# Equal dense shares for steps with a PV pair, and LayerNorm roots taken four blocks at a time, in a fused attention and GLU kernel

## The chip, the cores and the metric

The kernel runs on one core of a Trainium2 chip. The metric is the device time of one execution in microseconds (us). Each kernel is run several times; medians and ranges of all runs are given. The span of a profile (first to last instruction) is some 1.7 us less than the time of the same execution.

PE is TensorE, ACT ScalarE, DVE VectorE, POOL GpSimd, SP the engine that issues most transfers.

## The reference, cut to what matters

```python
xn = layernorm(x)                      # x: 2048 x 640
q, k, v = split(xn @ wqkv)             # 32 heads of 20
p = softmax(mask(q @ k.T * 20**-0.5))  # causal, window of 256
A = (p @ v) @ wo
B = (sigmoid(xn @ w_gate) * (xn @ w_up)) @ w_down   # inner size 1536
return x + A + B
```

## The kernel before

The 2048 rows are four chunks of 512. Attention runs in 76 score steps: 16 for chunk 0, 20 for each of the others (four wide steps and a full one for every two groups of heads). A step is 16, 24 or 32 small score matmuls into one PSUM tile `ps`, one exponential over all of it on ACT, and masks on POOL. While ACT works, PE is fed from a queue of dense work ("fill"): projections, gate and up blocks, the down projection, the output projection. The PV products of two groups (`acc`, 2 x 28 matmuls in chunk 0, 2 x 48 later) come due at fixed steps.

```python
def scores(c, step):
    pt = pp.tile([P, HG, PTW], BF16, name="pT")
    ps = ps_s.tile([P, HG, CW], FP32, name="ps")      # one buffer
    ...                                               # score matmuls
    nc.scalar.activation(out=pt[:, :, 0:CW], in_=ps, func=EXP, scale=SCALE)
    ...                                               # three masks on GpSimd
```

The gate and up blocks: tanh on ACT writes `th`, of which there is one buffer; DVE makes `h` of it. Engines take their instructions in the order in which they were recorded, so where a block stands between the steps also fixes where its tanh and its h stand.

```python
tp = pool("tp", 1)
...
th = tp.tile([P, CW], FP32, name="th")
nc.scalar.activation(out=th, in_=pg, func=TANH, scale=0.5)
yield 5 * MM
...                                                   # five up matmuls into pu
nc.vector.scalar_tensor_tensor(out=h, in0=th, scalar=1.0, in1=pu, op0=ADD, op1=MULT)
yield 5 * MM
```

The loop that decides how much dense work a step gets. `fill.pull(ns)` emits pieces until their cost is at least `ns`; `PV` is the charge per PV group. After a PV pair DVE transposes both accumulators; scaling one group (reciprocal, products, a transpose) is emitted behind each of the next two pieces.

```python
PV = 740
...
for t, (c, k, step) in enumerate(todo):
    ...
    for group in due.get(t, []):
        pv(*group, parts.pop(group))
    made = (step, scores(c, step))
    ...
    sums = [PV * len(due.get(x, [])) for x in range(t + 1, min(last, len(todo) - 1) + 1)]
    credit += (fill.left(label) + sum(sums)) / (last - t) - sum(sums[:1])
    credit = fill.pull(credit)
```

A PV pair is emitted ahead of the next scores, so it lies at the end of a step, behind that step's dense work.

The softmax here doesn't subtract the row's maximum and nothing guards it: scores larger than these inputs give would overflow.

## Time and profile before

| | kernel before |
|---|---|
| time, median of 3 runs | 320.13 us (319.48 to 321.1) |
| profiled span | 317.9 us |
| PE / ACT / POOL / DVE busy | 96% / 61% / 51% / 50% |
| first and last score step begin at | 31.5 and 292.5 us |

The useful reading is by steps: the distance from the start of one step's first score matmul to the start of the next, less the price of the work in the step (the prices are worked out in the prediction below). What is over is PE's wait in that step. "Excess" below always means this.

### The profile page before, as it was taken

The numbers are of one execution on the slowest core, as the hardware profiler recorded it, in microseconds if no ns is written. First come the engines' busy times: TensorE is split into PE (matmuls) and PEld (weight loads), VectorE is DVE, ScalarE is ACT, GpSimd is POOL, SyncE is SP. The second block draws the span as 40 slices with busy tenths as digits, with TensorE's granted clock in tenths as the row PEclk, the third lists the DMA queues.
The fourth block names the chain that finished last, engine by engine and source line by source line (L and its number), as shares of the span: only waits on it lengthen the run. The fifth ranks groups of instructions, "written<-read, shape, count | busy, mean of one in ns | idle before, by whom it ended". The sixth has DMA issues, their size and how long they took to land.

```text
span 317.9 us, 10527 instructions
## 1 busy us (share of the span) xinstructions
PE 306.4 (96%) x4627; PEld 176.5 (56%) x4666; DVE 158.0 (50%) x313; ACT 192.6 (61%) x179; POOL 161.0 (51%) x257
## 2 busy tenths in 40 slices
PE   8999999999999999999999999999999999998996
PEld 2654444556567655554566656554466655453675
DVE  3531568637685344277651644345262717272054
ACT  5724878597754458766754457867667567868100
POOL 3000487667685554737565463735547474747000
PEclk9999999999999999999999999999999999999999
DMA  7985999537704254520424024600000010000002
GB/s 260 371 293 176 337 386 127 206 110 241 155 23 62 66 173 124 169 76 0 41 40 50 25 104 141 207 7 2 0 5 23 23 37 8 2 4 0 3 2 83
DMA packets 34669, 33.08 MB, mean 104 GB/s; under 512 B 10016, under 2 KB 34080, under 8 KB 34592
## 3 DMA queue, kind: packets, MB, share of 16 engines
q1 hardware_dynamic: 34192, 32.14, 35.8%
q8 instruction: 36, 0.59, 0.8%
q10 hardware_dynamic: 432, 0.28, 0.3%
q14 instruction: 9, 0.07, 0.1%
HBM read 21.00 MB, written 10.26 MB: 98 GB/s over the span
## 4 chain that ended last, share of the span: by engine, by line
PE 76%; ACT 10%; POOL 6%; issue 3%; DMA 3%; DVE 1%; ACTq 0%
PE y L416 14%; PE pqk L291 12%; PE pu L402 11%; PE pg L395 11%; ACT pT L469 8%; PE ps L464 7%; PE y L423 6%; PE pv L318 6%; PE acc L496 6%; POOL pT L472 5%; PE d L416 2%; DMA xnT<-xn 2%; POOL rstd L258 1%; DMA xc<-in_A_x_dram 1%; PE d L423 1%
## 5 line engine op out<-in xcount | busy, mean ns | idle before, releaser
L472 POOL TENSOR_SCALAR_AFFINE_SELECT pT<-pT 128x512 bf16<-128x512 bf16 (+2 forms) x192 | 146.8, 796 | 131.0 <-ACT pT L469 130.9
L469 ACT ACTIVATE pT<-ps 128x2048 bf16<-128x2048 f32 x76 | 142.7, 1878 | 68.6 <-PE ps L464 63.8
L406 DVE SCALAR_TENSOR_TENSOR h<-th,pu 128x512 bf16<-128x512 f32 x48 | 32.9, 685 | 62.7 <-PE pu L402 37.7
L395 PE MATMUL pg<-xnT,wg 128*128 128x512 bf16 x224 | 58.3, 380 | 1.3 <-issue 0.6
L402 PE MATMUL pu<-xnT,wu 128*128 128x512 bf16 x227 | 58.8, 380 | 0.6
L416 PE MATMUL y<-wd,h 128*128 128x320 bf16 (+1 forms) x348 | 49.9, 297 | 0.0
L291 PE MATMUL pqk<-xnT,wqkv 128*128 128x512 bf16 x190 | 45.8, 381 | 0.7 <-DMA xnT<-xn 0.2
L416 PEld LDWEIGHTS <-h 128*128 128x128 bf16 x396 | 36.8, 98 | 14.3
L398 ACT ACTIVATE th<-pg 128x512 f32<-128x512 f32 x48 | 28.6, 595 | 17.1 <-PE pg L395 14.3
L464 PEld LDWEIGHTS <-kT 20*64 20x64 bf16 x1856 | 21.2, 103 | 27.2 <-issue 25.2
L402 PEld LDWEIGHTS <-wu 128*128 128x128 bf16 x240 | 22.0, 98 | 25.7 <-DMA wu<-in_B_w_up_dram 0.4
L464 PE MATMUL ps<-qT,kT 20*64 20x128 bf16 (+4 forms) x1856 | 32.5, 239 | 3.5 <-ACT pT L469 3.4
L395 PEld LDWEIGHTS <-wg 128*128 128x128 bf16 x240 | 21.7, 98 | 24.9 <-issue 0.6
L506 DVE STREAM_TRANSPOSE t<-acc 128x512 f32<-128x512 f32 x32 | 21.8, 708 | 23.9 <-PE acc L496 23.9
L291 PEld LDWEIGHTS <-wqkv 128*128 128x128 bf16 x200 | 22.3, 119 | 18.6 <-issue 1.5
L427 DVE SCALAR_TENSOR_TENSOR xn<-y,xc 128x320 bf16<-128x320 f32 (+1 forms) x29 | 14.0, 485 | 29.4 <-PE y L423 29.4
L518 DVE TENSOR_TENSOR on<-t,rec 128x320 bf16<-128x320 f32 (+4 forms) x48 | 27.2, 567 | 1.1
L496 PE MATMUL acc<-pT,v 128*32 128x64 bf16 (+3 forms) x1376 | 23.9, 223 | 1.4 <-ACT pT L469 1.1
L496 PEld LDWEIGHTS <-v 128*32 128x32 bf16 x1376 | 19.1, 97 | 9.2 <-issue 4.6
L318 PE MATMUL pv<-wqkv,xnT 128*128 128x320 bf16 x160 | 23.6, 299 | 0.0
L423 PE MATMUL y<-wo,oc 128*128 128x320 bf16 (+1 forms) x145 | 21.6, 297 | 0.0
L295 DVE CAST st<-pqk 128x512 bf16<-128x512 f32 x20 | 13.8, 691 | 12.6 <-PE pqk L291 12.6
(46 smaller groups left out, 151.1 us busy)
## 6 DMA issues: line engine op xcount, KB each, us to landing
qT<-sq SPq DMA_DIRECT2D x7, 512.0 KB, 5.8
sq<-st SPq DMA_DIRECT2D x20, 128.0 KB, 3.5
sk<-st SPq DMA_DIRECT2D x20, 128.0 KB, 2.7
out_dram<-xn SPq DMA_DIRECT2D x15, 160.0 KB, 1.8
kT<-sk SPq DMA_DIRECT2D x4, 512.0 KB, 6.7
wg<-in_B_w_gate_dram SPq DMA_DIRECT2D x2, 960.0 KB, 7.6
wu<-in_B_w_up_dram SPq DMA_DIRECT2D x2, 960.0 KB, 9.6
xc<-in_A_x_dram SPq DMA_DIRECT2D x3, 640.0 KB, 5.4
```

The source lines that it names most:

```text
L291: nc.tensor.matmul(ps, lhsT=wt[:, m, :], rhs=xnT[c][:, d, :], start=(d == 0), stop=(d == DC - 1))
L318: nc.tensor.matmul(ps[:, 0:HALF], lhsT=xnT[c][:, d, s * P:(s + 1) * P], rhs=wqkv[:, d, 2 * D + hf * HALF:2 * D + (hf + 1) * HALF], start=( ...
L395: nc.tensor.matmul(pg, lhsT=part(wg, d, f), rhs=xnT[c][:, d, :], start=(d == 0), stop=(d == DC - 1))
L398: nc.scalar.activation(out=th, in_=pg, func=TANH, scale=0.5)
L402: nc.tensor.matmul(pu, lhsT=part(wu, d, f), rhs=xnT[c][:, d, :], start=(d == 0), stop=(d == DC - 1))
L406: nc.vector.scalar_tensor_tensor(out=h, in0=th, scalar=1.0, in1=pu, op0=ADD, op1=MULT)
L416: nc.tensor.matmul(y[:, 0:cut[1] - cut[0]], lhsT=ht[c, f][:, s * P:(s + 1) * P], rhs=wd[:, f, cut[0]:cut[1]], start=(f == 0), stop=False)
L423: nc.tensor.matmul(y[:, 0:cut[1] - cut[0]], lhsT=oc[c, m][:, s * P:(s + 1) * P], rhs=wo[:, m, cut[0]:cut[1]], start=False, stop=(m == DC - 1))
L464: nc.tensor.matmul(ps[hf * U:(hf + 1) * U, i, col * U:(col + n) * U], lhsT=qk["k", kc, g // GH][32 * i:32 * i + DH, g % GH, key:key + U], ...
L469: nc.scalar.activation(out=pt[:, :, 0:CW], in_=ps, func=EXP, scale=SCALE)
L472: nc.gpsimd.affine_select(out=out, in_=in_, pattern=[[0, HG], [0, n], [sign, width]], compare_op=GE, fill=0.0, base=base, channel_multipli ...
L496: nc.tensor.matmul(acc[32 * i:32 * i + 32, q * U:(q + n) * U], lhsT=v[:, h * VW:h * VW + 32], rhs=pt[:, i, col * U:(col + n) * U], start=( ...
```

## The change

Its intent: give every score step of a stage the same dense work, whether it also has a PV pair or not; and take LayerNorm's reciprocal root once for four blocks instead of once per block, with the normalisation a piece of work later, so that DVE waits less for it.

```diff
-    def rstd_block(mv):
-        rstd = lnp.tile([P, 1], FP32, name="rstd")
-        nc.gpsimd.tensor_scalar(out=rstd, in0=mv[:, 1:2], scalar1=EPS, scalar2=None, op0=ADD)
-        nc.gpsimd.tensor_tensor(out=rstd, in0=rstd, in1=neghalf, op=POW)
-        return rstd
+    def rstd_blocks(mvs):
+        rstds = lnp.tile([P, SBC], FP32, name="rstds", bufs=1)
+        nc.gpsimd.tensor_scalar(out=rstds, in0=mvs[:, :, 1], scalar1=EPS, scalar2=None, op0=ADD)
+        nc.gpsimd.tensor_tensor(out=rstds, in0=rstds, in1=neghalf, op=POW)
+        return rstds
 ...
-        for k in range(SBC + 4):
-            ...   # statistics of block k, root of k-1, norm of k-3, turn of k-4
+        for s in range(SBC):
+            ln_block(c, s, mvs[:, s, :])
+            if s == SBC - 1:
+                rstds = rstd_blocks(mvs)
+            yield 0
+        yield 0
+        for s in range(SBC):
+            norm_block(c, s, mvs[:, s, :], rstds[:, s:s + 1])
+            yield 0
+            if turn:
+                turn_block(c, s)
 ...
-    PV = 740
 ...
-        sums = [PV * len(due.get(x, [])) for x in range(t + 1, min(last, len(todo) - 1) + 1)]
-        credit += (fill.left(label) + sum(sums)) / (last - t) - sum(sums[:1])
+        credit += fill.left(label) / (last - t)
         credit = fill.pull(credit)
```

(Cut: the signatures of the helpers, and the constant of -0.5 widened to four columns.)

More of the change, by code (lines that the diff above doesn't have):

```diff
@@ L225 @@
     make_identity(nc, ident)
-    neghalf = const.tile([P, 1], FP32, name="neghalf")
+    neghalf = const.tile([P, SBC], FP32, name="neghalf")
     nc.gpsimd.memset(neghalf, -0.5)
@@ L245, in ln_half, with ln_mv, ln_block @@
         return stats
-    def ln_mv(stats):
-        mv = lnp.tile([P, nc.vector.BN_AGGR_DIM], FP32, name="mv")
+    def ln_mv(stats, mv=None):
+        if mv is None:
+            mv = lnp.tile([P, nc.vector.BN_AGGR_DIM], FP32, name="mv")
         nc.vector.bn_aggr(out=mv, in_=stats)
         return mv
-    def ln_block(c, s):
-        return ln_mv(ln_half(c, s, 1, ln_half(c, s, 0)))
-    def rstd_block(mv):
-        rstd = lnp.tile([P, 1], FP32, name="rstd")
-        nc.gpsimd.tensor_scalar(out=rstd, in0=mv[:, 1:2], scalar1=EPS, scalar2=None, op0=ADD)
-        nc.gpsimd.tensor_tensor(out=rstd, in0=rstd, in1=neghalf, op=POW)
-        return rstd
+    def ln_block(c, s, mv=None):
+        return ln_mv(ln_half(c, s, 1, ln_half(c, s, 0)), mv)
+    def rstd_blocks(mvs):
[3 more added lines that the diff above has]
+        return rstds
     def norm_block(c, s, mv, rstd):
@@ L336, in g_norms @@
         new_xnT(c)
-        mv, rstd = {}, {}
-        for k in range(SBC + 4):
-            if k < SBC:
-                mv[k] = ln_block(c, k)
-            if 0 <= k - 1 < SBC:
-                rstd[k - 1] = rstd_block(mv[k - 1])
-            if k < SBC:
-                yield 0
-            if 0 <= k - 3 < SBC:
-                norm_block(c, k - 3, mv[k - 3], rstd[k - 3])
-                yield 0
-            if turn and 0 <= k - 3 - 1 < SBC:
-                turn_block(c, k - 3 - 1)
+        mvs = lnp.tile([P, SBC, nc.vector.BN_AGGR_DIM], FP32, name="mvs", bufs=1)
+        for s in range(SBC):
[9 more added lines that the diff above has]
+                turn_block(c, s)
     def g_turns(c):
@@ L634 @@
     proj_v(0, 3, 1, act)
-    nc.scalar.activation(out=scr, in_=neghalf, func=EXP)
+    nc.scalar.activation(out=scr, in_=neghalf[:, 0:1], func=EXP)
     for _ in g_qk(0):
```

## The prediction

> **What bounds the kernel now.** I read the page's totals first, then the waits of TensorE (PE), then the timeline around the steps in which PE stood still, and last the list of PE matmuls by form.
>
> ```profile
> PE 306.4 (96%) x4627; PEld 176.5 (56%) x4666; DVE 158.0 (50%) x313; ACT 192.6 (61%) x179; POOL 161.0 (51%) x257
> ...
> PEclk9999999999999999999999999999999999999999
> ...
> PE 76%; ACT 10%; POOL 6%; issue 3%; DMA 3%; DVE 1%; ACTq 0%
> ```
> PE is busy nearly all the time at full clock and has 76% of the chain that ended last; no other engine is over 61%. So only what PE does not fill can be won. How much is that? The waits give the kind:
> ```profile
> PE ps L464 <- ACT pT L469: 3.4, 5, 1.3
> ...
> PE acc L496 <- ACT pT L469: 1.1, 4, 0.5
> ...
> ACT th L398 <- DVE h L406: 1.0, 1, 1.0
> ```
> Five times the next scores (ps) wait for the exponential (pT), because ps has one buffer; four times the PV product (acc) waits for it. PE's idle time is understated, since a matmul's end is modelled and overlaps the next: the mean of a 512-column matmul is 380 ns, yet five of them take 1.08 us in the chain, 0.216 each. So I measured from starts. Each of the 76 score steps is: scores, exponential on ScalarE (ACT), masks on GpSimd (POOL), and dense work on PE meanwhile. From the timeline a step without waits is 0.46 us for scores and switching, plus 0.216 per 512-column matmul, 0.136 per 320-column one, plus 1.46 for a PV pair of chunks 1 to 3 (2 x 48 matmuls) or about 1.1 for one of chunk 0 (2 x 28). That sum reproduces most of the 75 step lengths to 0.02 us. Where it does not, PE waited:
> ```profile
> 244.14 0.43 PE L464 MATMUL ps<-qT,kT 20*64 20x128 bf16 x32
> 244.50 0.99 PE L416 MATMUL y<-wd,h 128*128 128x320 bf16 x6
> 244.73 1.88 ACT L469 ACTIVATE pT<-ps 128x2048 bf16<-128x2048 f32 x1 [1.02 <-PE ps L464]
> 245.42 0.74 PE L496 MATMUL acc<-pT,v 128*32 128x320 bf16 x40
> 246.66 0.97 PE L496 MATMUL acc<-pT,v 128*32 128x128 bf16 x56 [0.50 <-ACT pT L469]
> 247.56 0.44 PE L464 MATMUL ps<-qT,kT 20*64 20x320 bf16 x24
> ```
> This PV step has six dense matmuls. Its last 56 PV matmuls read the exponential of the same step (done at 246.61), so the step lasts 3.42 us for 2.74 of work: 0.68 idle. The other kind, in the last chunk:
> ```profile
> 268.74 0.59 DVE L518 TENSOR_TENSOR on<-t,rec 128x256 bf16<-128x256 f32 x1
> 269.25 0.68 DVE L406 SCALAR_TENSOR_TENSOR h<-th,pu 128x512 bf16<-128x512 f32 x1
> 270.02 0.60 ACT L398 ACTIVATE th<-pg 128x512 f32<-128x512 f32 x1 [1.02 <-DVE h L406]
> 270.51 1.87 ACT L469 ACTIVATE pT<-ps 128x2048 bf16<-128x2048 f32 x1
> 272.44 0.43 PE L464 MATMUL ps<-qT,kT 20*64 20x320 bf16 x24 [0.60 <-ACT pT L469]
> ```
> VectorE (DVE) scaled the two PV groups before it got to h; th has one buffer, so tanh waited for h; the exponential stands behind tanh and came late; PE stood.
>
> Step by step, the waits before are: thin steps (dense work under the 2.56 us that scores plus exponential take) 0.74 + 0.44 + 0.46 = 1.64; PV steps with too little dense work 0.14 + 0.42 + 0.68 + 0.42 + 0.36 = 2.02; the DVE lag above, twice, 0.68 + 1.42 = 2.10; the two steps around the normalisation of chunk 1, 0.55; scattered rest 0.47. Together 6.8 us, 2% of the time: a ceiling on the gain.
>
> **What the Trainium skill says.** "Perfetto Trace Analysis", Identifying the Most-Contended Engine, warns that matmul busy share does not tell how near PE is to its limit because matmuls are pipelined; the trace agrees (380 ns booked, 216 ns spacing). The same page, Tensor Engine Instruction, calls ACT, DVE and GPSIMD strict FIFO; the tanh at 270.02 holding up the exponential at 270.51, whose scores had been issued by 269.4, agrees. "SBUF — State Buffer", Who interferes with whom, says a DVE instruction with two SBUF inputs contends with a GpSimd instruction that reads SBUF; the 320-column scaling takes 0.49 us where it starts before the masks (235.10) and 0.95 under them (250.19), which fits, though it does not prove it. "GPSIMD Engine Reference", Elementwise — side-by-side cycle accounting, names two software dispatch hops per instruction; the trace has 0.593 us for a power of one column, so I take that as nearly all fixed.
>
> **The change part by part.**
> Shares. The matmuls are the same, 4666 on both sides; only their places move. The old rule charged 740 ns per PV group against a step's share, so PV steps got little dense work (one block of five) and the others two or three blocks. The new rule gives all steps of a stage the same dense work, PV or not. I took the new PE order from the instruction listing and priced every step with the constants above.
> - PV steps of chunks 1 to 3 now hold at least 10 wide or 16 narrow dense matmuls: at least 0.46 + 2.16 + 1.46 = 4.08 us, above the 3.42 floor. The 2.02 goes to 0.
> - Thin steps: three become two, one with ten 320-column matmuls (1.82 of work, 0.74 idle), one with twelve (2.09, 0.46): 1.64 to 1.20.
> - Last chunk: each step becomes gate block, up block. After a PV step the DVE order is then two transposes, scaling, h, scaling, h, instead of h, both scalings (3.0 and 3.7 us), h. From PV end at A: the transposes end at A+0.84, the first scaling by A+2.8, h at A+3.8, the second scaling by A+5.8, h at A+6.5; the tanh that needs that buffer stands behind an exponential that ends at about A+7.7. No wait: 2.10 to 0. The plain steps here are 2.62 us against a floor of 2.56, so the margin is only 0.06.
> LayerNorm. Twelve pairs on POOL (12 x (0.224 + 0.593) = 9.8 us) become three. With four columns in place of one I estimate 0.85 a pair, 2.6 in all: 7.2 us off POOL, which at 51% is not the bound, so worth nothing directly. But the norms come about two dense pieces later. In chunk 1 the root now waits for all four statistics and for the masks of the next step: exponential done 43.0, masks to 45.0 (1.95), root to 45.85, first norm to 46.35 instead of 43.63. h of that pair is queued behind it (47.05), and tanh, so the next exponential slips 0.2. Then the last two norms and the scalings of chunk 0's first pair share DVE: norm 49.35, h 50.05, scaling 51.0, norm 51.45, scaling 53.7, h 54.4. The tanh before the next exponential waits to 55.05, where scores are ready at 53.85: about 1.1 us of PE idle. With the 0.1 before it, 1.2. The four transposing DMAs (first issued at 43.66 before, about 2.1 us apart, last landed 56.08) start near 46.4; PE wants them at about 57.2 by then. I allow 0.3. So 0.55 becomes 1.5.
> Slots: in two places an output tile now follows at once on the add that frees its PSUM buffer, without scores between: 0.1 each; with the old rest, 0.7.
> Sum after: 1.20 + 0 + 0 + 1.5 + 0.7 = 3.4, against 6.8. Saved 3.4 of 320.13: **316.7 us**, 1.1% less. Head and tail (before the first scores at 31.5, after the last at 292.5) are untouched.
>
> **Rivals.**
> 1. The new chunk-1 wait is larger: transposes finish in DMA order behind the 1.9 MB load of wd, whose packets run to about 49.5, and three of four landings came after 54. If SP issues them from 46.4 at 2.1 us each and the last lands 5.6 us after its issue at 52.7, PE waits 1 us more: 317.7 to 318.5. For it: PE already waited 0.2 for the last one. Against: in chunks 2 and 3, without such a load, issue takes 1.25 and landing 2.6.
> 2. The uniform 2.62 us steps become bound by the exponential: ACT has 1.88 + 0.60 per step plus the hand-over of 0.66 (end of exponential to start of the next), so any tanh that overhangs by over 0.06 us lengthens the step. Over ten steps at 0.1 that is 1 us: 317.7. Against: nine such two-block steps before ran at 2.62.
> 3. Only the shares matter and the norms cost nothing, as POOL's relief (four root pairs fell between masks at 42.6 to 47.8 before) lets PV masks finish early: then the 1.5 returns to 0.3 and it is 315.5.
> 4. Nothing gained, because work moved from PV steps makes other steps thin. The priced list speaks against it: only two steps are under 2.56.
>
> **Range and chances.** Runs of the kernel before spread 1.6 us. Rivals 1 and 2 together give 319, rival 3 and a little luck 315. Range 314.9 to 319.0. Faster by over 2% needs 313.7, less than a full removal of all but 0.4 us of waits: 3%. Slower by over 2% needs over 6 us of new waits: 2%. Within 2%: 95%.
>
> **What would show it.** Right: no wait of acc for the exponential; PV steps of about 4.1 us; no tanh waiting for h in the last chunk, where step lengths repeat 2.62 and 4.08; six root instructions on POOL, about 2.6 us in all; two steps of 2.56 in the third out-projection; a tanh near 54 that waits for h, and a late exponential after it. Wrong: first QK projection of chunk 1 waiting over 1 us for the transposes; last-chunk steps above 2.7; a DVE that waits for the root longer than the 6.5 us of before with PE idle behind it.

## The result, and the profile after

The changed kernel takes **316.19 us** (median of 4 runs, 315.95 to 317.66), the kernel before 320.62 (4 runs, 319.48 to 321.52) in the same rounds. The ratio is 0.9873, 95% interval 0.9827 to 0.992: within 2%. A ratio is the mean time of one kernel's fast runs over that of the other's of the same rounds, so it is not quite the ratio of the medians. The prediction was 316.7, range 314.9 to 319.0. The two profiled spans differ by 3.2 us: 3.0 of it is excess in the steps, 0.2 an earlier start (first scores at 31.3 us in place of 31.5). The medians differ by 4.4, so some 1 us between them is not in these two profiles.

The totals and the chain that ended last, from the page of the changed kernel:

```profile
span 314.7 us, 10543 instructions
...
PE 307.0 (98%) x4666; PEld 175.7 (56%) x4666; DVE 157.6 (50%) x313; ACT 192.6 (61%) x179; POOL 154.7 (49%) x239
...
PE 91%; ACT 4%; POOL 1%; DMA 1%; issue 1%; DVE 1%; ACTq 0%
```

Busy times moved by less than 1 us but for POOL's 6; what changed is the chain, which runs through PE for 91% of the span where it was 76%. PE's waits in the changed kernel (who waited for whom: us in total, times, longest):

```profile
PE ps L464 <- ACT pT L469: 1.9, 3, 0.8
PE pwarm L235 <- DVE st L164: 1.3, 1, 1.3
PE pt L272 <- DVE xn L264: 0.7, 1, 0.7
PE y L416 <- issue: 0.6, 1, 0.6
PE pu L402 <- DVE h L406: 0.3, 1, 0.3
```

The wait of `acc` for the exponential is gone. Five waits of the scores are three: two thin steps and one near chunk 1's norms. New are a wait of 0.6 for "issue", of which more below, one for h, and one in the start (`pt` for `xn`). The kernel before had four waits for "issue", of 0.2 at most, all at `pg`, of whose 240 matmuls 16 are missing from its trace. A PV step of the last chunk and the step after it, from the timeline of the changed kernel:

```profile
260.09 0.43 PE L464 MATMUL ps<-qT,kT 20*64 20x128 bf16 x32
260.45 1.25 PE L395 MATMUL pg<-xnT,wg 128*128 128x512 bf16 x5
260.69 1.88 ACT L469 ACTIVATE pT<-ps 128x2048 bf16<-128x2048 f32 x1 [1.54 <-PE ps L464]
261.54 1.24 PE L402 MATMUL pu<-xnT,wu 128*128 128x512 bf16 x5
...
262.72 1.52 PE L496 MATMUL acc<-pT,v 128*32 128x320 bf16 x96
...
264.17 0.43 PE L464 MATMUL ps<-qT,kT 20*64 20x320 bf16 x24
...
266.79 0.43 PE L464 MATMUL ps<-qT,kT 20*64 20x320 bf16 x24
```

The exponential ends at 262.57, before the first PV matmul at 262.72, so all 96 run in one go, where the kernel before had a break between 40 and 56 of them. The step lasts 4.08 us, the next 2.62; both are their work to 0.01.

Two steps near chunk 1's norms are over their work, by 0.54 and 0.92 us. The second, in the same timeline:

```profile
50.92 1.22 DVE L264 TENSOR_SCALAR xn<-xc,mvs,rstds 128x640 bf16<-128x640 bf16 x1
...
53.37 0.48 DVE L518 TENSOR_TENSOR on<-t,rec 128x128 bf16<-128x128 f32 x1
...
53.77 0.67 DVE L406 SCALAR_TENSOR_TENSOR h<-th,pu 128x512 bf16<-128x512 f32 x1
53.78 1.25 PE L395 MATMUL pg<-xnT,wg 128*128 128x512 bf16 x5
54.54 0.60 ACT L398 ACTIVATE th<-pg 128x512 f32<-128x512 f32 x1 [1.76 <-DVE h L406]
...
55.03 1.87 ACT L469 ACTIVATE pT<-ps 128x2048 bf16<-128x2048 f32 x1
...
56.95 0.42 PE L464 MATMUL ps<-qT,kT 20*64 20x320 bf16 x16 [0.84 <-ACT pT L469]
```

It is the picture that the prediction showed for the last chunk of the kernel before, moved here: DVE is at a norm and at the scaling, h comes at 53.77, tanh waits for h, the exponential stands behind tanh, the next scores wait for the exponential.

One wait was not foreseen. PE and its weight loads (PEld) in the step at 88 us of the changed kernel:

```profile
88.37 0.45 PE L416 MATMUL y<-wd,h 128*128 128x320 bf16 x2
...
89.43 0.39 PEld L416 LDWEIGHTS <-h 128*128 128x128 bf16 x4 [0.95 <-issue]
89.43 0.72 PE L416 MATMUL y<-wd,h 128*128 128x320 bf16 x4 [0.62 <-issue]
```

In the middle of a group of twelve matmuls, whose operands had all been there for long, even the weight load stops until 89.43; no semaphore is named. The step is 0.79 us over its work.

Excess by kind in the profiles of both kernels, in us, beside what was predicted of the changed one:

| | before | predicted after | after |
|---|---|---|---|
| thin steps | 1.64 | 1.20 | 1.17 |
| PV steps | 2.02 | 0 | 0 |
| DVE lag, last chunk | 2.10 | 0 | 0 |
| near chunk 1's norms | 0.55 | 1.5 | 1.46 |
| step at 88 us | 0 | not foreseen | 0.79 |
| rest | 0.47 | 0.7 | 0.33 |
| sum | 6.78 | 3.4 | 3.75 |

### The profile page after: what moved, and what is told of

It reads as the page before. It is cut to its first block, busy times and chain, and to the rows that moved or that the text cites.

```text
span 314.7 us, 10543 instructions
## 1 busy us (share of the span) xinstructions
PE 307.0 (98%) x4666; PEld 175.7 (56%) x4666; DVE 157.6 (50%) x313; ACT 192.6 (61%) x179; POOL 154.7 (49%) x239
## 4 chain that ended last, share of the span: by engine, by line
PE 91%; ACT 4%; POOL 1%; DMA 1%; issue 1%; DVE 1%; ACTq 0%
PE pg L395 16%; PE pu L402 15%; PE y L416 15%; PE pqk L292 14%; PE ps L464 8%; PE pv L319 7%; PE acc L496 7%; PE y L423 5%; ACT pT L469 4%; PE d L416 2%; DMA xc<-in_A_x_dram 1%; POOL pT L472 1%; PE d L423 1%; POOL rstds L259 0%; PE pt L272 0%
## 5 line engine op out<-in xcount | busy, mean ns | idle before, releaser
L402 PE MATMUL pu<-xnT,wu 128*128 128x512 bf16 x240 | 59.8, 380 | 0.3 <-DVE h L406 0.3
L395 PE MATMUL pg<-xnT,wg 128*128 128x512 bf16 x240 | 59.9, 380 | 0.0
L416 PE MATMUL y<-wd,h 128*128 128x320 bf16 (+1 forms) x348 | 50.6, 297 | 0.6 <-issue 0.6
L518 DVE TENSOR_TENSOR on<-t,rec 128x320 bf16<-128x320 f32 (+4 forms) x48 | 25.1, 523 | 1.1
L496 PE MATMUL acc<-pT,v 128*32 128x64 bf16 (+3 forms) x1376 | 23.0, 223 | 0.0
```

The lines of the kernel that those rows point to most:

```text
L395: nc.tensor.matmul(pg, lhsT=part(wg, d, f), rhs=xnT[c][:, d, :], start=(d == 0), stop=(d == DC - 1))
L402: nc.tensor.matmul(pu, lhsT=part(wu, d, f), rhs=xnT[c][:, d, :], start=(d == 0), stop=(d == DC - 1))
L416: nc.tensor.matmul(y[:, 0:cut[1] - cut[0]], lhsT=ht[c, f][:, s * P:(s + 1) * P], rhs=wd[:, f, cut[0]:cut[1]], start=(f == 0), stop=False)
L496: nc.tensor.matmul(acc[32 * i:32 * i + 32, q * U:(q + n) * U], lhsT=v[:, h * VW:h * VW + 32], rhs=pt[:, i, col * U:(col + n) * U], start=( ...
```

## The experiments

Three questions were open. Is it the shares or the LayerNorm part that earns the time? Are the three mechanisms (the floor of PV steps, tanh behind h, thin steps) causes or only companions? What is the wait at 88 us? The theory is the prediction's; the main rival is that relief of POOL by the batched roots earns a good part. Four kernels ran on one chip, three on a second, two on a third, five rounds each but for one with three; all gave correct results.

### Shares alone

```diff
-    PV = 740
+    PV = 0
```

on the kernel before. With a charge of 0 the formula is that of the changed kernel, and the listing of PE's instructions is that of the changed kernel, one by one.

> Kernel before with the PV charge set to 0 (equal dense shares), LayerNorm as before; its PE order is that of the changed kernel matmul for matmul. Theory (the shares earn everything, the LayerNorm part costs about 1 us in chunk 1): waits of 1.2 in two thin steps, none in PV steps, none for tanh behind h in the last chunk, 0.3 to 0.5 near the norms of chunk 1: 4.5 to 5 us under the kernel before, about 1 us under the changed kernel. Rival (relief of POOL by the batched roots earns a good part): only 2 us or less under the kernel before, slower than the changed kernel.

Measured: 316.44 us (315.71 to 316.94), before 319.93 (319.06 to 321.03, 11 runs); ratio 0.9891, interval 0.9871 to 0.9911. That is 3.5 us, less than the 4.5 to 5 expected, but nearly all of what the whole change earns (0.9873 and, in the repeat below, 0.9888); the time is not 1 us under that of the changed kernel. PV steps have no excess and the DVE lag in the last chunk is gone; thin steps have 1.17. Two things were missed: the step at 88 us has 0.42 here as well, and the two steps near the norms have 0.29 and 0.58, 0.87 in all, although LayerNorm is the old one. From the table of waits between 44 and 58 us of this kernel:

```profile
ACT th L398 <- DVE h L406: 2.5, 2, 1.7
```

So tanh waits for h here without any change to LayerNorm. The shares alone put "up, gate" into the steps right after chunk 0's first PV pair. Of the two waits the longer, 1.71 us before a tanh at 51.03, is for an h that stands on DVE behind a norm (49.78), which had itself waited 1.04 us for its root; the other, 0.83 us before a tanh at 54.23, is for an h that stands behind both scalings.

### LayerNorm alone

The changed kernel with the old charge put back:

```diff
+    PV = 740
-        credit += fill.left(label) / (last - t)
+        sums = [PV * len(due.get(x, [])) for x in range(t + 1, min(last, len(todo) - 1) + 1)]
+        credit += (fill.left(label) + sum(sums)) / (last - t) - sum(sums[:1])
```

PE's instructions are those of the kernel before, one by one.

> Changed kernel with the old share rule (740 ns charged per PV group), new LayerNorm; PE order of the kernel before. Theory: all waits of the kernel before stay (PV steps 2.0, DVE lag 2.1, thin 1.6) and about 1 us is added near chunk 1's norms (tanh waiting for h): 0.5 to 1.5 us slower than before. Rival: 1 to 3 us faster than before through POOL's relief.

Measured: 319.51 us (319.34 to 320.17), before 319.93; ratio 0.9994, interval 0.9975 to 1.0013. It earns nothing and costs nothing. The rival falls: POOL is relieved and the time does not move. My own expectation of 0.5 to 1.5 us slower falls too: near the norms the excess is 0.26, less than the 0.55 before. The old waits are all there, as in the last chunk of this kernel:

```profile
270.41 0.60 ACT L398 ACTIVATE th<-pg 128x512 f32<-128x512 f32 x1 [1.01 <-DVE h L406]
```

### Two buffers for tanh's output, in the kernel before

```diff
-    tp = pool("tp", 1)
+    tp = pool("tp", 2)
-            th = tp.tile([P, CW], FP32, name="th")
+            th = tp.tile([P, CW], BF16, name="th")
```

Two tiles in bf16 take the room of one in fp32; two in fp32 did not fit.

> Kernel before with two buffers for tanh's output, in bf16 so that they fit. Theory: in the last chunk tanh no longer waits for h, so the two late exponentials (0.68 and 1.42) go; PV steps stay at 3.42 and thin steps at 2.55: 2.1 to 2.3 us faster than before. Rival (the exponential waits for the GpSimd masks, as the table of waits books it): unchanged within 0.3.

Measured: 317.77 us (316.95 to 318.96), ratio 0.9942, interval 0.9919 to 0.9966: 1.9 us faster by the ratio. The excess of the two late steps in the last chunk went from 0.68 and 1.42 to 0; the 2.02 in PV steps and 1.64 in thin steps stayed. The same place in the timeline:

```profile
268.15 0.59 DVE L518 TENSOR_TENSOR on<-t,rec 128x256 bf16<-128x256 f32 x1
...
268.66 0.67 DVE L406 SCALAR_TENSOR_TENSOR h<-th,pu 128x512 bf16<-128x512 bf16 x1
268.66 0.60 ACT L398 ACTIVATE th<-pg 128x512 bf16<-128x512 f32 x1 [0.22 <-PE pg L395]
```

tanh no longer waits for h: both start at 268.66. The rival, that the exponential waits for the masks as the table of waits books it (4.4 us for POOL in the kernel before), falls: POOL's work is untouched and the delay is gone. The booking named the semaphore that came last; the thing that held was the buffer. The change of type is no rival: an h takes 685 ns on average with fp32 and with bf16 `th`.

### The same in the changed kernel

The same two lines in the changed kernel.

> Changed kernel with two buffers for tanh's output, in bf16. Theory: the two long steps around chunk 1's norms (0.54 and 0.92 over their work) lose most of their wait, 1.2 us faster than the changed kernel. Rival (they are long because PE or ACT waits for the roots or for the transposes): unchanged within 0.3.

Measured: 315.91 us (314.95 to 317.04), ratio to before 0.9876, interval 0.9852 to 0.99. The time is that of the changed kernel within noise (316.19 and 316.98 on other chips), so by time the expectation of 1.2 us failed. In the profile the mechanism held: near chunk 1's norms the excess is 0.21 in place of 1.46, and the DVE still waits for the roots (2.8 us) as before, so the long steps come from tanh behind h and not from the roots. What was won there was lost elsewhere in this execution: 0.59 in a step at 40.6 us, where PE waited for the second half of `w_up`, and 1.02 in the step at 88 us. Whether two buffers help the changed kernel is not settled by this run.

### The floor of PV steps: a larger charge

```diff
-    PV = 740
+    PV = 1110
```

on the kernel before.

> Kernel before with the PV charge raised from 740 to 1110 ns, so that PV steps get hardly any dense work. The floors (2.55 us for a plain step, 3.42 for a PV step of chunks 1 to 3) priced on its PE order give 11.6 us of waits against 3.7 for the kernel before: theory: 6.5 to 8.5 us slower than before, with every PV step of chunks 1 to 3 at 3.42 us (six of dense work or less). Rival (PV steps do not matter, only the DVE lag does): within 1.5 us of before.

Measured: 326.42 us (325.31 to 327.6, 4 runs), before 319.77 (319.18 to 323.81); ratio 1.0188, interval 1.0132 to 1.0243: 6.7 us slower by the medians, in the range expected, and 6.0 by the ratio, a little under it. Of the eleven PV steps of chunks 1 to 3 nine last 3.36 to 3.46 us, the other two 3.54 and 4.12. One of the nine, in the timeline of this kernel, has no dense work at all:

```profile
99.69 0.43 PE L464 MATMUL ps<-qT,kT 20*64 20x128 bf16 x32
...
100.05 0.74 PE L496 MATMUL acc<-pT,v 128*32 128x320 bf16 x40
100.28 1.88 ACT L469 ACTIVATE pT<-ps 128x2048 bf16<-128x2048 f32 x1 [3.19 <-PE ps L464]
102.21 0.97 PE L496 MATMUL acc<-pT,v 128*32 128x128 bf16 x56 [1.42 <-ACT pT L469]
...
103.10 0.43 PE L464 MATMUL ps<-qT,kT 20*64 20x320 bf16 x24
```

With 1.92 us of work the step still lasts 3.42: it is scores, exponential, and 56 matmuls behind it. PE's wait in `acc` for the exponential is 8.3 us in this kernel, 1.1 in the kernel before, none in the changed one. The excess of these eleven steps goes from 2.02 to 10.0 us. The charge moves other work too: the DVE lag in the last chunk falls from 2.10 to 0.20, and one PV step of chunk 0 has 0.92. In all the excess is 13.3 us, 6.5 more than before. So the charge sets the time mostly through this floor.

### The wait at 88 us: the loads of wo earlier

In the changed kernel:

```diff
                 proj_block(w, c, m)
+                if c == 1 and w == "q" and m == 2:
+                    load_wo()
 ...
-    fill.add("wo", later(load_wo), 0)
```

The trace keeps the transfers of a queue named "instruction", in packets of 16 KB, 36 of them in the span. PE and its weight loads have some 9,330 records, about 260 per packet, which fits a program that PE reads as it runs. In the kernel before one such packet started at 84.3 us, in the changed kernel at 86.9, behind the loads of K, Q and wo. The DMA engines' load in the two kernels at that time (columns: stretch, its length, busy time of PE, PEld, DVE, ACT and POOL, granted clock, DMA share, GB/s), kernel before:

```profile
84.00:86.00 2.00, 2.00 (x85) 1.53 (x85) 1.73 (x3) 1.23 (x2) 0.90 (x2) 1.00 0.48 111
86.00:88.00 2.00, 2.00 (x17) 1.45 (x15) 1.93 (x4) 1.69 (x1) 1.92 (x4) 1.00 0.03 11
```

and changed kernel:

```profile
84.00:86.00 2.00, 2.00 (x85) 1.61 (x85) 1.60 (x3) 0.66 (x2) 2.00 (x3) 1.00 1.10 220
86.00:88.00 2.00, 2.00 (x16) 1.27 (x13) 1.90 (x7) 1.58 (x1) 0.63 (x2) 1.00 0.40 93
```

In the changed kernel the engines are full until about 86, in the kernel before until about 84, some 2 us less. PE stops after record 1984 or 1985. Over the five traces that have all 9352 PE records, the number of records PE had done when the packet landed, against its excess in that step:

| profile | packet started, us | PE records done at its landing | excess, us |
|---|---|---|---|
| LayerNorm alone | 85.4 | 1908 | 0 |
| two buffers, before | 84.9 | 1914 | 0 |
| shares alone | 85.9 | 1930 | 0.42 |
| changed kernel | 86.9 | 1957 | 0.79 |
| two buffers, after | 86.7 | 1973 | 1.02 |

The later the packet against PE's progress, the longer the wait. PE's weight loads, of which every trace has all 4666, say the same with more traces: 947 of them were done at the landing in the kernel before and 952 in the last kernel below (excess 0), 951 and 954 in the first two rows (0), 962 with the shares alone (0.42), 962 in the changed kernel run again (0.46), then 979 and 987 (0.79 and 1.02). In the four traces with a wait PE stops after the same weight load and goes on 1.3 to 1.5 us after the landing.

> Changed kernel with the four loads of wo issued inside the Q projection of chunk 1 (near 63 us) instead of behind the K and Q loads of chunk 1 (78 to 80 us). Theory: PE stood 0.79 us in the step at 88 us because the fetch of its program came late behind these loads (16 KB at 86.9 us, 84.3 before); with the loads gone the fetch comes by about 85 and the wait there goes: step at its work of 3.44 us, 0.4 to 0.9 us faster than the changed kernel. Rival (the wait belongs to that place in the PE order): it stays.

Measured: the excess in that step is 0 in the profile. The packet did not start by 85 us but at 86.5; PE ran some 3 us late by then, for a reason that follows, and had done 873 weight loads at the landing, not 979. So in this profile PE's lateness helped as well; the last two kernels below, which also load wo early, have the packet at 84.8 and 84.2 us and no excess there either. The time does not show the gain: 317.4 us (315.77 to 319.15, six runs in two clusters, 315.8 to 316.4 and 318.4 to 319.2), ratio 0.9905, interval 0.9853 to 0.9956. The profiled execution was the slowest (319.15): one step at 40.6 us is 3.73 over its work. Two things make this up, a wait and then a stretch at half clock (columns of the second line as above):

```profile
PE pu L404 <- DMA wu<-in_B_w_up_dram: 2.0, 1, 2.0
...
43.30:46.70 3.40, 3.40 (x10) 1.14 (x8) 0.91 (x2) 0.00 (x0) 3.06 (x5) 0.50 1.05 399
```

PE waits 2.0 us for the second half of `w_up`; then the ten 512-column matmuls of the step run at a granted clock of 0.50 for 3.4 us, which costs another 1.7. No other profile here has such a stretch among its score steps. Whether the wait brought it is not shown: it began 0.3 us after the wait ended, but a wait of 1.5 us in another profile (the changed kernel again, below) had none behind it.

The last packet of the second halves of the gate and up weights ended at 42.55 us here, at 39.5 in the changed kernel's profile, at 40.9 with two buffers and 38.6 in the last kernel below. This load comes before anything that this edit touches, so I take the spread as one of executions. One half-clock stretch of 3.4 us lowers the mean clock of a run to 0.995 (worked out from this profile: 3.41 x 0.5 of 317 us). The second run of the upper cluster (318.58, clock 0.994) fits that; so do four outliers elsewhere, each the slowest of its series, at 0.995: 323.81 and 323.26 of the kernel before, 319.49 and 319.69 of two kernels below. The third of the cluster (318.39, clock 0.999) does not, and no trace of these others was kept.

### A candidate: no step under 2.1 us of dense work

Shares alone, with two bf16 buffers for tanh and wo early, and

```diff
-        credit = fill.pull(credit)
+        credit = fill.pull(max(credit, 2100))
```

> Candidate: equal shares and the LayerNorm of before, two bf16 buffers for tanh's output, wo loaded early, and no step given less than 2.1 us of dense work. Theory: no thin step, no PV step at its floor, no tanh behind h: waits of 0.3 to 1 us in all, so 2.5 to 3.3 us under the changed kernel: 312.9 to 313.7 us. Rival (steps of two blocks are bound by the exponential once nothing else is): 315 or more, with step lengths over 2.64 throughout the last chunk.

Measured: 316.6 us (315.79 to 319.49), ratio 0.9895, interval 0.9841 to 0.995. A miss by 3 us. The last chunk is as hoped, each step at its work, so the exponential does not bind steps of 2.62 us. But in chunk 0 PE waits 1.04 us at a PV pair between V projections and 0.52 in the next step, for PSUM tiles that DVE still reads (the kernel before has a PV pair between V projections too, without this wait, so what brings it is not shown); and its start (first scores at 32.4 us, not the 31.3 to 31.7 of most profiles here) was slow in the profiled execution.

### The changed kernel again

Unchanged, on the chip of the next run.

> The changed kernel once more, as the measure for the next run on the same chip and as a second look at its waits. Theory: steps again at their work but for the two thin ones (0.71, 0.46), the two near chunk 1's norms (about 0.5 and 0.9) and the one at 88 us (0.4 to 1.0, the late program fetch); 1.0 to 1.5% faster than before. If the wait at 88 us were chance, it would be missing here.

Measured: 316.98 us (315.79 to 319.69), before 320.45 (319.15 to 323.26); ratio 0.9888, interval 0.9847 to 0.9929. The step at 88 us has 0.46, so it is no chance, but its size varies. Near the norms there is 0 and 0.62 this time. A step at 40.4 us is 1.47 over: here the `w_up` packets ended at 41.7 us and its weight load waited 1.5 us for them. The slowest run (319.69) has a clock of 0.995.

### The floor in the last chunk alone

The candidate with the floor confined to the last chunk:

```diff
-        credit = fill.pull(max(credit, 2100))
+        credit = fill.pull(max(credit, 2100) if c == NCH - 1 else credit)
```

> Candidate as floor_2100, but with the 2.1 us floor in the last chunk's steps alone, so that chunk 0 keeps the equal shares and its PSUM order: the waits at 69 and 74 us of floor_2100 (1.04 and 0.52) should go. Theory: no thin step, no wait at 88 us, at most 0.3 near chunk 1's norms: waits of 0.5 to 0.9 us against 3.7 of the changed kernel, 2 to 3 us under it. Rival (what is won step by step is lost in the start, whose loads vary from run to run): under 1 us.

Measured: **315.0 us** (314.46 to 316.08), ratio to before 0.9829, interval 0.9796 to 0.9861. Against the changed kernel on the same chip (316.98) it is 2.0 us by the medians, at the low end of what was expected. Its profile:

```profile
span 312.7 us, 10521 instructions
...
PE 305.2 (98%) x4628; PEld 175.5 (56%) x4666; DVE 159.4 (51%) x313; ACT 193.1 (62%) x179; POOL 161.1 (52%) x257
```

The excess is 0.6 us in all: 0.21 near the norms, 0.09 at the V projections, none at 88 us and no thin step. It keeps the old LayerNorm and is faster than both kernels; its four edits were not timed one by one, so what each earns is not shown.

Excesses of six profiles, in us (one execution each; "rest" is 0.02 in many steps). The three that are left out have sums of 13.3 (charge of 1110), 5.92 (wo early) and 1.86 (floor everywhere):

| | shares alone | LayerNorm alone | two th, before | two th, after | after again | floor last |
|---|---|---|---|---|---|---|
| thin steps | 1.17 | 1.64 | 1.64 | 1.17 | 1.17 | 0 |
| PV steps | 0 | 2.02 | 2.02 | 0 | 0 | 0 |
| DVE lag, last chunk | 0 | 2.09 | 0 | 0 | 0 | 0 |
| near chunk 1's norms | 0.87 | 0.26 | 0 | 0.21 | 0.62 | 0.21 |
| step at 88 us | 0.42 | 0 | 0 | 1.02 | 0.46 | 0 |
| late w_up | 0 | 0 | 0 | 0.59 | 1.47 | 0 |
| rest | 0.33 | 0.56 | 0.48 | 0.33 | 0.32 | 0.41 |
| sum | 2.79 | 6.57 | 4.14 | 3.32 | 4.04 | 0.62 |

## Why the prediction was right

The time lies 0.5 us under the prediction, inside the range. The two large terms, PV steps and DVE lag, were right in mechanism and size. That the rest came out too is partly luck: 0.5 us foreseen for transposes and slots did not come, 0.79 not foreseen did, and the term for the norms had the right size from a wrong cause. By its steps:

- **The ceiling.** That PE bounds the kernel and that only 6.8 us of waits could be won held. The kernel that removes almost all of them has 0.6 left and is about 5.5 us faster by the medians.
- **PV steps.** 2.02 to 0, as said. The charge of 1110 ns, which takes their excess to 10.0, shows that the floor is a cause.
- **DVE lag in the last chunk.** 2.10 to 0, as said; shown by the two buffers, which remove it from the kernel before at the same PE order.
- **Thin steps.** 1.20 said, 1.17 found, in the two steps named. The floor of 2.1 us takes them to 0, but only together with other edits, so their share of the time was not shown alone.
- **LayerNorm.** The sum was right (1.5 said, 1.46 found) by luck, for the step that gave it failed in its cause: "in chunk 1 the root now waits for all four statistics" was to cost about 1.2 us, and LayerNorm alone costs nothing (0.9994). The first norm did come at 46.04 and the late tanh at 54.54, near the 45.9 and 55.05 worked out, but with the old LayerNorm the shares already leave 0.87 there. The later norms add to a DVE queue that the shares made long: 0.59 more in one pair of profiles, 0.25 less in the other. What LayerNorm adds to the time is not resolved; it is under what the runs can tell. Rival 3 is right that the norms alone cost nothing, but not that the 1.5 would then be 0.3.
- **The root's size.** "Nearly all fixed" was wrong: the power of four columns takes 1.045 us, not about 0.6. A pair is 0.228 + 1.045 = 1.27 us where 0.85 was estimated. It moved nothing, since POOL does not bind.
- **Transposes.** The 0.3 us did not come, and rival 1 fell with it: PE did not wait for a transpose. The four landed 2.6 to 3.9 us after issue, 5.6 to 7.9 before; in the repeat of the changed kernel it was 4.0 to 6.5, without a wait either. That they met fewer packets of the load of wd, being issued later, was not tested.
- **Slots.** The 0.2 us for output tiles behind their adds did not come; both steps are at their work.
- **Not foreseen.** The wait of 0.4 to 1.0 us at 88 us took the place of these. The order of eight traces, the restart at a fixed time after the landing and the move of wo point to the fetch of PE's program behind other transfers; the fetch itself was not varied alone.
- **Rivals 2 and 4.** In the last chunk the two stretches of four two-block steps, on either side of a PV step, ran at 2.62 us each, so the exponential does not bind them with 0.06 us of margin; and only two steps are thin.

## What to carry to other kernels

When one engine is nearly full, price each step of the schedule by its own work from start-to-start distances and list only the steps that are longer: the list was 6.8 us long and told what could be won, where the share of busy time could not. Before a slow execution is put down to a wait, its granted clock should be read stretch by stretch: a mean of 0.995 hid 1.7 us here. Work that must wait for the step's own result (here PV behind the exponential) should lie behind as much independent work as other steps have, so charging it against that step's share is the wrong way round. And a single buffer between two in-order engines turns a late step of one into a stop of everything behind it on the other.

## What the Trainium skill lacked or had wrong

- "Runtime: NRT & Kernel Launch", Instruction fetch mechanics, says that an engine's program is refilled in 16 KiB blocks over a DMA queue and that the cost of crossing a block is "mostly hidden". Where data transfers filled the DMA engines (share 1.10 between 84 and 86 us) PE stood 0.42 to 1.02 us in one step, without a branch, and went on 1.3 to 1.5 us after a block had landed late; with the transfers moved the wait was 0. That the block held PE's program is inferred.
- "GPSIMD Engine Reference", Elementwise — side-by-side cycle accounting, gives the cost of an add per element and of dispatch. A power is far from that: 0.593 us for one column and 1.045 for four on 128 partitions, 0.15 us per added column.
- No page read has how far the arrival of a large load differs between executions of one program: the last packet of the second halves of the gate and up weights ended between 38.6 and 42.6 us over the profiles here, and PE waited 0 to 2.0 us for it.
